# The clamp of the weights' scaled upper words: on GpSimd in place of VectorE, in a fused attention and MLP kernel

## The chip, the cores and the metric

The kernel runs on one core of a Trainium2 chip. The metric is the device time of one execution in microseconds (us), as a median over runs. Five engines work side by side, each through its own instruction queue, in order: TensorE (PE in the rows, PEld for its weight loads), VectorE (DVE), ScalarE (ACT), GpSimd (POOL) and SyncE (SP), which issues the DMAs here.

## The reference

Attention with a narrow band (16 positions to each side) and one summary per block of 32 keys, then an MLP with h * tanh(softplus(h)) over its output. The weights `w_in` (512 x 2048) and `w_out` (2048 x 512) come in as 64-bit floats and have to be made into 32-bit ones.

```python
scores_l = scale * np.matmul(q, k.transpose(0, 1, 3, 2))      # kept where |i - j| < 16
scores_s = scale * np.einsum('bhsd,bhnd->bhsn', q, k_sum) + np.log(32)   # k_sum: maximum of each 32 keys
a = softmax(concatenate([scores_l_m, scores_s]))
x = a @ concatenate([v, v_sum])                               # v_sum: mean of each 32 values
h = x @ w_in
g = h * np.tanh(log1p(exp(h)))
out = g @ w_out
```

q, k and v have shape (4, 8, 768, 64); the MLP works on 3072 tokens of 512 features.

## The kernel before

Tokens are worked on in groups of 512. Attention comes in units (numbered 0, 1, 2, ... after the first ones, a0 to b3), each a pair of heads and 256 tokens: scores on TensorE (`S`), masked maxima on VectorE from PSUM (`ttr`, L380), exponents on ScalarE (`exp`, L393), the divisors (`rs`, L407 and L408), the normalizing product on GpSimd (`nm`, `att_normalize`, L412), a transpose on TensorE (`T`, L418), and the product with the values (`X`, L444). For the scores of a unit GpSimd also copies the block maxima of its keys next to the queries (`kc`, `att_key_summary`, L324).

The MLP runs each product three times on split numbers, upper part and remainder: `ph` (L516) is the first product for one block of 128 hidden features, and needs both words of `w_in`; ScalarE applies the activation and makes the upper part (`ah`, L532), VectorE the remainder (`al`, L534); `po` (L544) is the second product, which needs `ah`, `al` and both words of `w_out`.

The weights come as 16 pieces of 128 x 1024 64-bit words, `w_in` and `w_out` in turn, numbered 0 to 15, and each is turned into 32-bit words by eight steps: `lw` loads it; `f` (L172) scales the upper halves on ScalarE into a tile `w_f` of which there is one; `B` (L176) shifts the lower halves and `C` (L180, the masking) adds the sign bit, both on VectorE and on another tile; `cl` (L184) is the clamp of `w_f`; `E` (L189, the join) brings the two together on VectorE; `hi` (L194) rounds the upper word on ScalarE and `G` (L197) makes the lower word by a subtraction on VectorE. The next piece's `f` waits for `G`, since the tile is free then. The lower words go to `w_early_in`, `w_early_out_lo`, `w_late_in` or `w_late_out_lo`.

The order of the instructions up to about 150 us is a list of words written out by hand, such as

```python
        ... C9 f9 po6 cl9 nm13 lt13 E9 lw11 hi9 pc12 B10
        al7 G9 kc15 f10 ph8 C10 mi8 xl11 ph9 cl10 po7 kc14 mi9 ah8 E10 S14 hi10 ...
```

and each engine takes its instructions in the order in which they stand there. After that stretch the kernel goes on with sums of the weights and products by a seven-product scheme for the later groups; no clamp is left by then.

Of the kernel before, what the change touches and what calls it, by code (L numbers as in the profile page):

```python
# [14 lines left out]
ALU = mybir.AluOpType  # L15
# [48 lines left out]
F32_MAX = (0x47EFFFFF - (OFFSET << 23))  # L64
# [3 lines left out]
def _as_f32(bits):  # L68
    import struct
    return struct.unpack("<f", struct.pack("<I", bits))[0]  # L70
# [3 lines left out]
def fused_kernel(ctx: ExitStack, tc: tile.TileContext, q0, qk, kt, v0, vw, vs, w_in, w_out, out):  # L74
    nc = tc.nc
# [38 lines left out]
    for h in range(2):  # L114
        r = slice(h * QT, (h + 1) * QT)
        nc.gpsimd.affine_select(
            out=base[r, 0:KW], in_=base[r, 0:KW], pattern=[[1, KW]], base=-1,
            channel_multiplier=-1, compare_op=ALU.is_ge, fill=NEG / SCALE)
        nc.gpsimd.affine_select(
            out=base[r, 0:KW], in_=base[r, 0:KW], pattern=[[-1, KW]], base=2 * WIN - 1,  # L120
# [32 lines left out]
    raw, floats = {}, {}  # L153
# [27 lines left out]
                                       op0=ALU.bitwise_and, op1=ALU.bitwise_or)  # L181

    def clamp_weight(k):
        nc.vector.tensor_scalar(out=floats[k], in0=floats[k], scalar1=-_as_f32(F32_MAX), scalar2=_as_f32(F32_MAX),  # L184
                                op0=ALU.max, op1=ALU.min)

    def join_weight(k):
        u = floats[k].bitcast(U32)
# [19 lines left out]
    for part, step, at0 in ((blocks[:, :NW], QT, -WIN), (blocks[:, NW:], P, TG)):  # L208
        n = part.shape[1]
        nc.gpsimd.affine_select(  # L210
            out=part, in_=part, pattern=[[step, n], [-BLK, NB]], base=at0, channel_multiplier=1,
            compare_op=ALU.is_ge, fill=0.0)
        nc.gpsimd.affine_select(
            out=part, in_=part, pattern=[[-step, n], [BLK, NB]], base=BLK - 1 - at0, channel_multiplier=-1,
# [3 lines left out]
        out=part, in_=part, pattern=[[0, NW], [0, NB]], base=-WIN, channel_multiplier=1,  # L218
        compare_op=ALU.is_ge, fill=0.0)
    nc.gpsimd.affine_select(  # L220
        out=part, in_=part, pattern=[[0, NW], [0, NB]], base=WIN + QT - 1, channel_multiplier=-1,
# [461 lines left out]
    def summary_of(name):  # L683
# [10 lines left out]
        "vm": number(first_value_sums), "vc": number(first_value_summary),  # L694
        "lw": number(load_weight), "f": number(scale_weight), "B": number(low_bits), "C": number(sign_bits),
        "cl": number(clamp_weight), "E": number(join_weight), "hi": number(upper_weight),
        "G": number(lower_weight),
        "ph": step(ff_in), "mi": step(ff_act), "ah": split_of, "al": lambda name: lowers.pop("a" + name)(),
# [661 lines left out]
```

## Time and profile before

| | |
|---|---|
| median of 3 runs | 610.29 us (610.21 to 610.61) |
| the profiled execution | 608.81 us, of which the traced span is 606.9 us |
| TensorE busy | 589.2 us (97%) |
| VectorE busy | 452.1 us (75%) |
| ScalarE busy | 386.5 us (64%) |
| GpSimd busy | 80.7 us (13%) |
| granted TensorE clock | 0.996 of 2.4 GHz, mean |

The shares are means over stages with different limits: in the first 140 us, where the weights are made, VectorE is nearly full; later it is not. The rows that follow therefore look at that stretch, at what waits for what in it, and at how the clamp's neighbours stand.

### The profile page before, as it was taken

What the parts mean: (1) busy time and instruction counts of PE and PEld (TensorE: products, weight loads), DVE (VectorE), ACT (ScalarE), POOL (GpSimd) and SP (SyncE); (2) the same over time, 40 slices, a digit from 0 to 9 for tenths busy, and PEclk for the clock granted to TensorE, in tenths of its full rate; (3) what the DMA queues carried; (4) which work ended last, traced back from release to release, by engine and by line L of the source; (5) the groups of instructions that cost most, each with busy time, mean ns of one, the idle gap of its engine ahead of it and who ended that gap; (6) DMA issues with size and microseconds to landing.
All of it is one profiled execution on the core that took longest, in us unless ns stands there. A gap on an engine that the chain in (4) does not pass through costs nothing.

```text
span 606.9 us, 13906 instructions
## 1 busy us (share of the span) xinstructions
PE 589.2 (97%) x5142; PEld 527.4 (87%) x5142; DVE 452.1 (75%) x1158; ACT 386.5 (64%) x990; POOL 80.7 (13%) x119
## 2 busy tenths in 40 slices
PE   3999999999999999999999999999999999999997
PEld 3787777778788888998989898899999999999997
DVE  4999999998677768457786475879488787675565
ACT  3987586785446636588857885885346555666552
POOL 4531211300022012012102210221000000000000
PEclk9899999999999999999999999999999999999999
DMA  9978667653777898398998877697889989797753
GB/s 278 263 258 273 218 194 269 207 198 119 253 267 224 278 301 281 108 370 305 332 350 307 283 259 274 226 322 249 304 307 348 303 300 325 258 335 278 280 183 105
DMA packets 70964, 160.71 MB, mean 265 GB/s; under 512 B 10096, under 2 KB 23152, under 8 KB 70896
## 3 DMA queue, kind: packets, MB, share of 16 engines
q1 hardware_dynamic: 70896, 159.82, 77.8%
q8 instruction: 41, 0.67, 0.5%
q14 instruction: 27, 0.22, 0.1%
HBM read 130.42 MB, written 27.26 MB: 260 GB/s over the span
## 4 chain that ended last, share of the span: by engine, by line
PE 79%; DVE 7%; ACT 2%; issue 1%; DVEq 0%
PE po L544 24%; PE ph L816 14%; PE m L1031 13%; PE inner L1133 12%; PE ph L516 9%; PE x_ps L444 3%; PE pt_ps L418 3%; PE sc L359 3%; DVE w L180 1%; DVE al L534 1%; DVE w L176 1%; DVE w_f L184 1%; DVE w_f L189 1%; DVE w_early_out_lo L197 1%; ACT pr L393 0%
## 5 line engine op out<-in xcount | busy, mean ns | idle before, releaser
L412 POOL TENSOR_TENSOR pr<-pr,rs 128x480 f32<-128x480 f32 x48 | 57.1, 1190 | 278.5 <-DVE rs L408 246.4
L393 ACT ACTIVATE pr<-pr,nm 128x120 f32<-128x120 f32 x192 | 73.8, 388 | 10.3 <-DVE nm L380 10.0
L544 PE MATMUL po<-w_early_out_hi,ah 128*128 128x512 f32 x160 | 63.7, 398 | 0.0
L544 PE MATMUL po<-w_early_out_hi,al 128*128 128x512 f32 x160 | 62.4, 390 | 0.9 <-DVE al L534 0.9
L544 PE MATMUL po<-w_early_out_lo,ah 128*128 128x512 f32 x160 | 62.1, 388 | 0.0
L516 PE MATMUL ph<-xh,w_early_in 128*128 128x512 f32 x160 | 52.0, 391 | 0.0
L534 DVE TENSOR_TENSOR al<-h,ah 128x512 fp32r<-128x512 f32 x32 | 21.8, 690 | 38.3 <-ACT ah L532 38.3
L816 PE MATMUL ph<-xh,w_early_in 128*128 128x256 f32 x272 | 49.3, 276 | 0.0
L1133 PE MATMUL inner<-xh,w_early_in 128*128 128x256 f32 x240 | 49.1, 279 | 0.0
L816 PEld LDWEIGHTS ph<-xh,w_early_in 128*128 128x128 f32 x272 | 42.3, 187 | 0.6
L1133 PEld LDWEIGHTS inner<-xh,w_early_in 128*128 128x128 f32 x240 | 39.5, 187 | 0.1
L544 PE MATMUL po<-w_late_out_hi,ah 128*128 128x512 f32 x96 | 38.3, 399 | 0.0
L523 ACT ACTIVATE a<-ph 128x512 f32<-128x512 f32 x32 | 19.0, 599 | 30.0 <-PE ph L516 29.5
L816 PE MATMUL ph<-xl,w_early_in 128*128 128x256 f32 x136 | 37.4, 275 | 0.0
L544 PE MATMUL po<-w_late_out_lo,ah 128*128 128x512 f32 x96 | 37.3, 388 | 0.0
L544 PE MATMUL po<-w_late_out_hi,al 128*128 128x512 f32 x96 | 37.2, 388 | 0.0
L393 ACT ACTIVATION_READ_ACCUMULATOR pr<-pr,nm 128x1 f32 x192 | 36.6, 190 | 0.0
L544 PEld LDWEIGHTS po<-w_early_out_hi,al 128*128 128x128 f32 x160 | 30.1, 188 | 6.8 <-DVE al L534 2.1
L544 PEld LDWEIGHTS po<-w_early_out_lo,ah 128*128 128x128 f32 x160 | 30.0, 188 | 6.2
L516 PEld LDWEIGHTS ph<-xh,w_early_in 128*128 128x128 f32 x160 | 30.0, 188 | 6.1
L544 PEld LDWEIGHTS po<-w_early_out_hi,ah 128*128 128x128 f32 x160 | 30.0, 188 | 5.6 <-issue 0.8
L380 DVE CUSTOM_DVE_ANT_0 pr<-sc,base 128x120 f32<-128x120 f32 x128 | 31.4, 277 | 4.0 <-PE sc L359 2.6
(268 smaller groups left out, 1711.5 us busy)
## 6 DMA issues: line engine op xcount, KB each, us to landing
w_early_in<-w_sums SPq DMA_DIRECT2D x32, 1024.0 KB
w_early_in<-w_sums SPq DMA_DIRECT2D x32, 768.0 KB
qk<-qk SPq DMA_DIRECT2D x40, 496.0 KB
w<-w_in SPq DMA_DIRECT2D x16, 512.0 KB
w<-w_out SPq DMA_DIRECT2D x16, 512.0 KB
w_sums<-results SPq DMA_DIRECT2D x32, 256.0 KB
vw<-vw SPq DMA_DIRECT2D x40, 192.0 KB
w_late_in<-w_out_sums SPq DMA_DIRECT2D x25, 256.0 KB
```

The source lines that it names most:

```text
L359: nc.tensor.matmul(ps[h][row, at0:at0 + KA], u["qk"][r, s, h * QT:(h + 1) * QT], u["qk"][r, s, P:], start=True, stop=True)
L380: nc.vector.tensor_tensor_reduce(out=pr[:, j, :], in0=ps[h][:, at + pair * KA:at + (pair + 1) * KA], in1=m, scale=-SCALE, scalar=-NEG, op0 ...
L393: nc.scalar.activation(pr[:, s, :], pr[:, s, :], AF.Exp, scale=-1.0, bias=nm[:, s:s + 1], accum_out=sm[:, s:s + 1])
L412: nc.gpsimd.tensor_mul(u["p"], u["p"], u["r"].unsqueeze(2).broadcast_to([P, NQ, KA]))
L418: nc.tensor.transpose(ps[:KA, s * P:(s + 1) * P], u["p"][:, s, :], ident)
L516: nc.tensor.matmul(turned(ph), w[:, cc * P:(cc + 1) * P], turned(x[:, cc, :]), start=(cc == 0 and n == 0), stop=(cc == NCC - 1 and n == 2))
L523: nc.scalar.activation(a, st[g, fc], AF.Mish)
L534: return lambda: nc.vector.tensor_sub(al, a, ah.bitcast(F32))
L544: nc.tensor.matmul(turned(po[g][t]), a[:, tok], turned(w), start=(fc == 0 and n == 0), stop=(fc == NFC - 1 and n == 2))
L816: nc.tensor.matmul(turned(ps), w_[:, a * P:(a + 1) * P], turned(x[:, a, :]), start=(begins and a == 0 and n == 0), stop=(a == 1 and n == 2 ...
L1031: nc.tensor.matmul(turned(ps), a_[:, tok], turned(w_), start=(begins and n == 0), stop=(n == 2), skip_group_check=True)
L1133: nc.tensor.matmul(turned(ps), w_[:, a * P:(a + 1) * P], turned(x[:, a, :]), start=(begins and a == 0 and n == 0), stop=(a == 1 and n == 2 ...
```

## The change

`clamp_weight(k)` is issued on GpSimd in place of VectorE. The two bounds change places: the upper one is applied first. The words of the list stay where they are.

```diff
     def clamp_weight(k):
-        nc.vector.tensor_scalar(out=floats[k], in0=floats[k], scalar1=-_as_f32(F32_MAX), scalar2=_as_f32(F32_MAX),
-                                op0=ALU.max, op1=ALU.min)
+        nc.gpsimd.tensor_scalar(out=floats[k], in0=floats[k], scalar1=_as_f32(F32_MAX), scalar2=-_as_f32(F32_MAX),
+                                op0=ALU.min, op1=ALU.max)
```

On VectorE the 16 clamps leave the queue and nothing else moves. Here is one place, that of piece 3 (`w_2_743` is the tile of its 64-bit words, `w_f` that of the scaled ones):

```order
 L176 TENSOR_SCALAR w_2_743<-w_2_743 128x1024
 L180 SCALAR_TENSOR_TENSOR w_2_743<-w_2_743 128x1024
-L184 TENSOR_SCALAR w_f<-w_f 128x1024
 L189 SCALAR_TENSOR_TENSOR w_f<-w_f,w_2_743 128x1024
 L284 TENSOR_REDUCE km_1_916<-ks_1_852 128x24
```

The masking (L180) and the join (L189) now follow each other; the join still needs the clamp's result.

On GpSimd the clamps come between normalizing products (L412, `pr`) and copies of key maxima (L324, `qk`). Here is the place of clamps 8 to 14; `pr_1_1130` is the product of unit 13, `pr_3_1419` of 15, `pr_2_1408` of 14, and the copies are for units 15, 14, 16 and 17:

```order
+L184 TENSOR_SCALAR w_f<-w_f 128x1024 x2
 L412 TENSOR_TENSOR pr_1_1130<-pr_1_1130,rs_1_1288 128x480
 L324 COPY qk_3_1281<-km_3_1095 128x4x24
+L184 TENSOR_SCALAR w_f<-w_f 128x1024
 L324 COPY qk_2_1222<-km_2_1273 128x4x24
+L184 TENSOR_SCALAR w_f<-w_f 128x1024
 L412 TENSOR_TENSOR pr_3_1419<-pr_3_1419,rs_3_1474 128x480
+L184 TENSOR_SCALAR w_f<-w_f 128x1024
 L324 COPY qk_0_1509<-km_0_793 128x4x24
+L184 TENSOR_SCALAR w_f<-w_f 128x1024
 L412 TENSOR_TENSOR pr_2_1408<-pr_2_1408,rs_2_1512 128x480
 L324 COPY qk_1_1529<-km_1_916 128x4x24
```

The products and copies keep their order among themselves, and each now stands behind the clamps ahead of it: the copy for unit 14 (`qk_2_1222`) behind clamp 10, the product of unit 14 (`pr_2_1408`) and the copy for unit 17 behind clamp 13.

## Rows read from the trace of the kernel before

**Rows 1.** Busy time of each engine in stretches (us), instructions, granted clock, DMA share, GB/s.
```profile
30.00:135.00 105.00, 102.40 (x792) 82.64 (x792) 102.09 (x204) 77.09 (x162) 21.34 (x20) 1.00 0.70 234
135.00:450.00 315.00, 315.00 (x2652) 276.01 (x2649) 222.51 (x633) 198.78 (x521) 44.81 (x60) 1.00 0.79 271
```

**Rows 2.** Waits of TensorE and VectorE, 30 to 135 us: total, times, longest.
```profile
PE po L544 <- DVE al L534: 0.9, 3, 0.4
...
DVE al L534 <- ACT ah L532: 0.8, 2, 0.5
```

**Rows 3.** Timeline: start, duration (us), engine, line, instruction [idle before <- releaser].
```profile
101.55 0.68 DVE L534 TENSOR_TENSOR al<-a,ah 128x512 fp32r<-128x512 f32 x1
102.28 0.49 PE L544 MATMUL po<-w_early_out_hi,al 128*128 128x512 f32 x1 [0.44 <-DVE al L534]
...
121.57 0.72 PE L516 MATMUL ph<-xh,w_late_in 128*128 128x512 f32 x2 [0.46 <-DVE w_late_in L197]
...
133.94 1.42 DVE L197 TENSOR_TENSOR w_late_in<-w_f,w_late_in 128x1024 fp32r<-128x1024 f32 x1
135.81 0.39 PE L516 MATMUL ph<-xh,w_late_in 128*128 128x512 f32 x1
```

**Rows 4.** Timeline: GpSimd beside VectorE at four places.
```profile
23.37 2.91 POOL L412 TENSOR_TENSOR pr<-pr,rs 128x480 f32<-128x480 f32 x2 [3.74 <-DVE rs L407]
25.36 0.94 DVE L284 TENSOR_REDUCE km<-ks 128x24 f32<-128x768 f32 x1
...
59.98 1.96 POOL L324 COPY qk<-km 128x96 f32<-128x96 f32 x2 [6.40 <-DMA qk<-qk]
...
66.41 1.20 DVE L197 TENSOR_TENSOR w_early_out_lo<-w_f,w_early_out_hi 128x1024 fp32r<-128x1024 f32 x1
66.64 1.81 POOL L412 TENSOR_TENSOR pr<-pr,rs 128x480 f32<-128x480 f32 x1 [4.70 <-DVE rs L408]
67.52 1.48 DVE L176 TENSOR_SCALAR w<-w 128x1024 uint32<-128x1024 uint32 x1
```

**Rows 5.** One tile's instructions on GpSimd: shortest, median, longest (ns), first and last start.
```profile
L412 POOL TENSOR_TENSOR pr<-pr,rs x48: 985/987/1967, 14.4 to 415.5; 128x480 f32<-128x480 f32 x48
```

**Rows 6.** Timeline: piece 3 from ScalarE's scaling to the join.
```profile
46.30 1.19 ACT L172 ACTIVATE w_f<-w 128x1024 f32<-128x1024 f32 x1
46.84 0.69 DVE L176 TENSOR_SCALAR w<-w 128x1024 uint32<-128x1024 uint32 x1
47.56 1.23 DVE L180 SCALAR_TENSOR_TENSOR w<-w 128x1024 uint32<-128x1024 uint32 x1
48.71 0.69 DVE L184 TENSOR_SCALAR w_f<-w_f 128x1024 f32<-128x1024 f32 x1
49.43 1.23 DVE L189 SCALAR_TENSOR_TENSOR w_f<-w_f,w 128x1024 uint32<-128x1024 uint32 x1
```

**Rows 7.** GpSimd's groups by shape: count | busy us, mean ns of one | idle before.
```profile
L210 POOL TENSOR_SCALAR_AFFINE_SELECT blocks<-blocks 128x192 f32<-128x192 f32 x1 | 0.4, 397 | 0.1
...
L207 POOL MEMSET blocks<- 128x240 f32 x1 | 0.3, 298 | 0.0
...
L210 POOL TENSOR_SCALAR_AFFINE_SELECT blocks<-blocks 128x48 f32<-128x48 f32 x1 | 0.2, 232 | 0.0
...
L122 POOL MEMSET base<- 128x24 f32 x1 | 0.1, 118 | 0.1
```

**Rows 8.** Timeline: clamps 0 and 13, the product of unit 14, a late second product.
```profile
18.70 1.48 DVE L184 TENSOR_SCALAR w_f<-w_f 128x1024 f32<-128x1024 f32 x1
...
114.36 1.88 POOL L412 TENSOR_TENSOR pr<-pr,rs 128x480 f32<-128x480 f32 x1 [2.05 <-DVE rs L408]
115.31 1.48 DVE L534 TENSOR_TENSOR al<-a,ah 128x512 fp32r<-128x512 f32 x1
...
122.77 0.69 DVE L184 TENSOR_SCALAR w_f<-w_f 128x1024 f32<-128x1024 f32 x1 [0.65 <-ACT w_f L172]
...
147.85 0.49 PE L544 MATMUL po<-w_late_out_hi,ah 128*128 128x512 f32 x1
```

## The prediction

> **What bounds the kernel now.** I read the stretches first, since the clamps lie in the first 140 us alone. From 135 to 450 us TensorE has no idle time at all, so what it loses before 135 us stays lost. From 30 to 135 us TensorE is busy 102.40 and VectorE 102.09 of 105 us [rows 1]: there the two run level, and all but the first two and the last clamp lie there. The question is which of the two the other waits for.
>
> The list of waits answers it: TensorE's largest is the second MLP product waiting for VectorE's `al`, 0.9 us in three waits [rows 2]. The timeline shows where: the product at 102.28 comes just behind the `al` of 101.55 (ended 102.23), the `ph` at 121.57 waits for a lower weight word, and at 135.81 TensorE needs the next lower weight word, which VectorE delivers at 135.36 [rows 3]. The margins are 0, 0 and 0.45 us. Whatever VectorE loses before 135 us is therefore paid by TensorE nearly in full, and what VectorE gains can give back only TensorE's idle time there, 105 - 102.40 = 2.6 us.
>
> **The change part by part.** It takes 16 instructions from VectorE, each worth some 0.65 us from its start to the next one's (0.72 where that one needs its result, as at 48.71 below), and puts 16 on GpSimd, which has the time (21.34 of 105 us busy [rows 1]). The orders of TensorE, ScalarE and SyncE stay, and no DMA is moved. Two things have to be priced: how long GpSimd takes, and what VectorE can do meanwhile.
>
> *VectorE does not go on freely.* A GpSimd product was started at 66.64 during a VectorE subtraction [rows 4]; alone it takes 0.99 us (the median of 48 [rows 5]). It ended at 68.45, which is 0.84 us after the subtraction's end (67.61). The shift that VectorE began at 67.52 took 1.48 us; the one of 46.84 took 0.69 [rows 6]. Two GpSimd copies of 96 elements, which should be shorter than the 397 ns that a selection over 192 takes [rows 7], took 1.96 us together at 59.98, beside VectorE's work on piece 4 and 5 [rows 4]. So a GpSimd instruction and a VectorE one of these kinds exclude each other, with one GpSimd input too, and the one that waits goes next. A GpSimd instruction of length L costs VectorE about L - 0.20 (0.79 for 0.99), and ends about L - 0.15 after VectorE lets go. A VectorE reduction is not held: that of 25.36 took its 0.94 us beside a GpSimd product that ran to 26.28 [rows 4].
>
> The Trainium skill (SBUF — State Buffer, section "Who interferes with whom") says which VectorE instructions are free of this: those with at most one SBUF input, outside the two-port modes. By that page the score maxima and the subtraction from PSUM go on beside a clamp as the reduction does; if they were held too, the sum below would be some 1 us higher. The trace agrees for the reduction.
>
> *The length L of one clamp on GpSimd* has no row. From below: a memset takes 118 ns for 24 elements and 298 for 240, 0.83 ns an element, so 1024 take 0.95 us. From above: the product of two inputs, 987 ns for 480 elements [rows 5], scaled with 0.1 us fixed: 1.99 us. The nearest row reads one tensor, does a little arithmetic and writes one: the selection, 232 ns for 48 elements and 397 for 192, 1.146 ns an element [rows 7]. I take 0.397 + 832 x 0.001146 = 1.35 us.
>
> *Seven clamps (numbers 2, 3, 4, 5, 7, 10, 14) stand in a bare chain.* Number 3 is shown [rows 6]: the scaled words are ready at 47.49, the masking runs from 47.56 to 48.79, the clamp follows, and the join starts at 49.43, 0.64 us after the masking's end. On GpSimd the clamp can run when the masking lets go, ends L - 0.15 later, and the join follows 0.05 us behind (as the `ph` at 121.57 follows VectorE). The join is late by L - 0.15 + 0.05 - 0.64 = 0.61 us. If GpSimd gets in before the masking, the masking is pushed back instead, by about the same. Seven times 0.61 is 4.3 us.
>
> *Four (6, 8, 9, 11) have other VectorE work to run beside them.* There VectorE loses L - 0.20 and saves a step of some 0.65: 0.50 us each, 2.0 us; number 8 less by 0.25, since a subtraction that reads PSUM runs beside it: 1.75 us.
>
> *Numbers 12 and 13.* In GpSimd's order the normalizing product of unit 14 now stands behind clamp 13. Today it runs at 114.36 and stalls the `al` of 115.31 (1.48 us, [rows 8]; that of 101.55 took 0.68). That 0.80 goes away there and comes back ahead of join 13. Today's clamp 13 waits 0.65 us for ScalarE [rows 8]; now the masking that stands behind it in the list fills that wait. The two clamps cost about 0.5 each: -0.80 + 0.80 - 0.65 + 1.0 = +0.35 us.
>
> *Numbers 0 and 1*, before 30 us. Clamp 0 is itself stalled by GpSimd today (1.48 us from 18.70 [rows 8]); VectorE can go on with score maxima that read PSUM. I work out some 0.9 us earlier there, most of it lost again at number 1, where ScalarE's scaling sets the time: -0.2 us.
>
> *Sum.* 4.3 + 1.75 + 0.35 - 0.2 = 6.2 us later for VectorE at 135 us. Of VectorE's own waits for `ah`, 0.8 us in two [rows 2], I let the smaller, 0.3, swallow some (the other is for work that TensorE feeds, and moves along), and 0.45 is the margin at 135.81. That leaves 5.45 us for TensorE. Clamp 15 will be about 1 us late as well, but its words are needed at 147.85 only [rows 8], 12 us behind those of piece 14, while VectorE takes some 7.5 us for a piece (16 pieces in 120 us). Against the profiled execution that is 608.81 + 5.45 = 614.3; the median of the three runs stands 1.48 above that execution, and I add to the median: 610.29 + 5.45 = **615.7 us**. A measurement of this kernel can tell about 0.2% (1.2 us) from no change.
>
> **Rivals.** (a) *The clamp streams at one element a cycle.* With L = 0.95, the bound from the memsets, the terms are 1.5 + 0.15 - 0.45 - 0.2 = 1.0, less 0.75: 0.2 us, 610.5 us, no change that can be told. For it speaks that min and max are light work; against it, that no row with an input comes near that rate. The Trainium skill (GPSIMD Engine Reference, section "Engine selection") calls one-input work on GpSimd roughly line-rate, which is this rival; its section "Elementwise — side-by-side cycle accounting" has 1.8 cycles an element as the best case of a tight loop, from which I estimate 1.54 us for 1024 elements, and by the same terms 618.2 us. No row here has this operation.
>
> (b) *A long clamp, or GpSimd's queue as the new bound.* With L = 1.99 the terms are 8.75 + 4.3 + 1.65 - 0.2 - 0.75 = 13.75: 624 us. The queue alone could do it as well: the copy of the key maxima for unit 14 now stands behind clamp 10, which can't end before about 101.0, while TensorE makes the scores that need it some 2 us before the product at 102.28; and the copy for unit 17 comes after the product of unit 14. By my count the first costs TensorE 0.1 us more than the late `al` does, and the second nothing; if both are dearer, 617 to 618 us.
>
> (c) *Faster.* GpSimd starts when ScalarE's scaling ends and runs beside VectorE instructions that leave it free. Joins then come 0.6 us earlier, and TensorE's 2.6 us of idle time shrink: 607.7 us at best. This needs L below 0.74, or no exclusion; the copies at 59.98 speak against both.
>
> **How the numbers follow.** Forecast (L from 1.1 to 1.65, about 612.5 to 619.5 us) 0.60; (b) 0.18; (a) 0.14; (c) 0.08. The likeliest gives 615.7. The range runs from 610.8, which leaves out (c) and a part of (a), to 621.5, which leaves out the upper part of (b), L above 1.8. By the sign: faster 0.07 and within 0.2% 0.12 from (c) and (a), slower 0.81.
>
> **What would show it.** GpSimd's clamp should take 1.2 to 1.5 us where nothing holds it, and longer by what is left of a masking where it waits. VectorE should be busy less by most of 16 x 0.69 us, and stand waiting for GpSimd ahead of joins, a wait that is absent today. TensorE's idle time from 30 to 140 us should grow from 2.6 to about 8 us, in waits for `al`, `w_late_in` and what follows from them; after 150 us nothing should differ but the offset. I am wrong if the clamp comes out near 0.95 or 2 us, if TensorE's added waits are for GpSimd's copies or products, or if VectorE's subtractions and maskings keep their times while clamps run beside them.

## The result, and the profile after

The changed kernel takes 614.61 us (median of 7 runs, 612.85 to 616.42) against 610.21 us before (7 runs, 609.58 to 610.98). The ratio is 1.0074 [1.0051, 1.0097], so it is slower by 4.4 us; 615.7 was forecast. Its profiled execution took 613.67 us with a span of 611.6 us, 4.86 and 4.7 us more than before.

The clamp itself comes first. This is its line in the profile after (shortest, median, longest in ns, first and last start, form), and who waited for it (total us, times):

```profile
L184 POOL TENSOR_SCALAR w_f<-w_f x16: 1033/1083/1590, 18.8 to 143.0; 128x1024 f32<-128x1024 f32 x16
...
  DVE w_f L189: 8.3, 8
```

Unhindered it takes 1.03 us, not 1.35. The join now waits for it in 8 of 16 pieces.

The stretches and waits that answer to [rows 1, 2], same columns:

```profile
30.00:135.00 105.00, 100.81 (x807) 80.96 (x800) 96.41 (x180) 74.51 (x151) 35.46 (x33) 1.00 0.71 230
135.00:450.00 315.00, 314.75 (x2646) 275.20 (x2643) 221.17 (x636) 200.96 (x529) 47.95 (x63) 1.00 0.80 270
```

```profile
PE po L544 <- DVE al L534: 1.6, 3, 0.8
PE x_ps L444 <- DMA vw<-vm: 1.3, 1, 1.3
PE sc L359 <- POOL qk L324: 1.0, 1, 1.0
...
DVE w_f L189 <- POOL w_f L184: 6.5, 7, 1.3
DVE al L534 <- ACT ah L532: 0.7, 2, 0.4
```

VectorE is busy 5.7 us less than in [rows 1], and stands 6.5 us of that stretch waiting for GpSimd, a wait that was absent. TensorE's idle time grows from 2.6 to 4.2 us, and 0.25 us is new behind 135 us; from 30 to 140 us it is 4.4 us, where the prediction looked for about 8. The wait of 1.3 us that is put down to a DMA stands in a second profile of the changed kernel as one for ScalarE's `a`, also 1.3 us; before, that wait was 0.8 us. So VectorE was relieved of work, and the engine that it feeds still came later.

How much of the 4.7 us of span is the change? The first score and the last addition of the result, first two rows of before, then two of after (start, duration, engine, line, instruction):

```profile
7.81 0.62 PE L363 MATMUL sc<-ks,q 64*64 64x96 f32 x8 [7.81 <-DMA q<-q]
602.61 0.69 DVE L1309 TENSOR_TENSOR results<-inner,x_blocks 128x512 f32<-128x512 f32 x1
```

```profile
8.64 0.62 PE L363 MATMUL sc<-ks,q 64*64 64x96 f32 x8 [8.64 <-DMA q<-q]
606.29 0.69 DVE L1309 TENSOR_TENSOR results<-inner,x_blocks 128x512 f32<-128x512 f32 x1
```

Between the two lie 594.80 us before and 597.65 after: 2.85 us. The first query arrived 0.83 us later in this execution, and the store of the result took 1.0 us longer behind the last addition; neither has a clamp near it. TensorE's added idle time from 30 us on (1.6 and 0.25 us) is not all of the 2.85 us: the join of piece 1, which ends near 33 us, is 0.6 us late already (its rows stand in the section on the prediction).

**A bare chain, piece 4**, answers to [rows 6]:

```profile
56.24 1.22 DVE L180 SCALAR_TENSOR_TENSOR w<-w 128x1024 uint32<-128x1024 uint32 x1
57.03 1.33 POOL L184 TENSOR_SCALAR w_f<-w_f 128x1024 f32<-128x1024 f32 x1 [6.93 <-ACT w_f L172]
58.33 0.98 POOL L412 TENSOR_TENSOR pr<-pr,rs 128x480 f32<-128x480 f32 x1
58.39 2.00 DVE L189 SCALAR_TENSOR_TENSOR w_f<-w_f,w 128x1024 uint32<-128x1024 uint32 x1 [0.93 <-POOL w_f L184]
60.31 0.68 DVE L534 TENSOR_TENSOR al<-a,ah 128x512 fp32r<-128x512 f32 x1
61.05 0.50 PE L544 MATMUL po<-w_early_out_hi,al 128*128 128x512 f32 x1 [0.84 <-DVE al L534]
```

The clamp is started at 57.03 while the masking runs, and ends at 58.36, 0.90 us after the masking (57.46), which is L - 0.13. The join follows 0.03 us behind: 0.93 us from the masking's end where it was 0.64, late by 0.29, that is L - 0.74. What was not in that term is the next row: the product that was queued behind the clamp goes next, and the join needs 2.00 us in place of 1.23. TensorE then waits for `al`. This stall is moved rather than new: in the kernel before, the same product ran at 52.28 and held the subtraction of piece 3 (2.00 us from 52.66, in place of some 1.2).

**Piece 3**, where GpSimd gets in ahead of the masking:

```profile
49.06 1.04 POOL L184 TENSOR_SCALAR w_f<-w_f 128x1024 f32<-128x1024 f32 x1 [6.62 <-ACT w_f L172]
49.15 2.03 DVE L180 SCALAR_TENSOR_TENSOR w<-w 128x1024 uint32<-128x1024 uint32 x1
51.28 1.23 DVE L189 SCALAR_TENSOR_TENSOR w_f<-w_f,w 128x1024 uint32<-128x1024 uint32 x1
52.42 0.95 DVE L284 TENSOR_REDUCE km<-ks 128x24 f32<-128x768 f32 x1
```

The masking takes 2.03 us instead of 1.23 [rows 6]: 0.80, or L - 0.24, against 0.72 that the clamp used to take there. The reduction, which would have run beside the clamp, stands behind the join.

The sum over the pieces, from the groups of lines from 30 to 145 us (count | busy us, mean ns of one | idle us before them, and what ended it), before and then after:

```profile
L189 DVE SCALAR_TENSOR_TENSOR w_f<-w_f,w 128x1024 uint32<-128x1024 uint32 x15 | 18.6, 1239 | 0.4
L180 DVE SCALAR_TENSOR_TENSOR w<-w 128x1024 uint32<-128x1024 uint32 x14 | 17.8, 1272 | 0.2
...
L184 DVE TENSOR_SCALAR w_f<-w_f 128x1024 f32<-128x1024 f32 x14 | 10.4, 744 | 0.8 <-ACT w_f L172 0.7
```

```profile
L180 DVE SCALAR_TENSOR_TENSOR w<-w 128x1024 uint32<-128x1024 uint32 x14 | 21.7, 1552 | 0.2
L189 DVE SCALAR_TENSOR_TENSOR w_f<-w_f,w 128x1024 uint32<-128x1024 uint32 x15 | 21.5, 1434 | 8.8 <-POOL w_f L184 8.3
```

VectorE is spared 10.4 us of clamps and 0.8 of waits ahead of them. It pays 3.9 us in maskings, 2.9 in joins and 8.4 in waits. The balance is 4.0 us against it, of which part is stalls by products that used to fall on other instructions, such as the one at piece 4.

### The profile page after: what moved, and what is told of

Its sections match the earlier page's. It is cut to its first block, busy times and chain, and to the rows that moved or that the text cites. A ratio compares the mean times of both kernels' runs of the same rounds, so it can differ in the third digit from the quotient of the medians.

```text
span 611.6 us, 13912 instructions
## 1 busy us (share of the span) xinstructions
PE 589.6 (96%) x5142; PEld 526.9 (86%) x5142; DVE 446.4 (73%) x1142; ACT 386.6 (63%) x990; POOL 97.9 (16%) x135
## 4 chain that ended last, share of the span: by engine, by line
PE 77%; DVE 5%; issue 3%; ACT 2%; POOL 1%; POOLq 0%; DVEq 0%; ACTq 0%
PE po L544 23%; PE ph L816 13%; PE m L1031 12%; PE inner L1133 12%; PE ph L516 8%; PE x_ps L444 3%; PE pt_ps L418 3%; PE sc L359 2%; POOL w_f L184 1%; DVE w L180 1%; ACT w_f L172 1%; DVE al L534 1%; DVE w_f L189 1%; DVE w L176 1%; ACT pr L393 0%
## 5 line engine op out<-in xcount | busy, mean ns | idle before, releaser
L412 POOL TENSOR_TENSOR pr<-pr,rs 128x480 f32<-128x480 f32 x48 | 54.8, 1142 | 234.5 <-DVE rs L408 209.9
L523 ACT ACTIVATE a<-ph 128x512 f32<-128x512 f32 x32 | 19.0, 595 | 30.7 <-PE ph L516 30.2
```

Of the source, the lines that this page charges most:

```text
L412: nc.gpsimd.tensor_mul(u["p"], u["p"], u["r"].unsqueeze(2).broadcast_to([P, NQ, KA]))
L523: nc.scalar.activation(a, st[g, fc], AF.Mish)
```

## The experiments

**First: how long may the clamp be?** Theory: the clamp shuts VectorE out for about L - 0.2 us, and what counts is whether that is more or less than the 0.65 us that the step takes on VectorE. Rival: GpSimd's queue, or something that comes with the change whatever L is. Four kernels on one chip: the change once more, without the clamp (it is left out, the words go on unclamped), with the clamp made twice, and on one half of the columns (the other half stays unclamped).

```diff
 def clamp_weight(k):          # change once more: as it is
-    nc.gpsimd.tensor_scalar(out=floats[k], in0=floats[k], ...)
+    pass                                                            # without
+    nc.gpsimd.tensor_scalar(...); nc.gpsimd.tensor_scalar(...)      # twice
+    nc.gpsimd.tensor_scalar(out=floats[k][:, :WP], in0=floats[k][:, :WP], ...)  # half
```

> The changed kernel once more, with a second profile. In the first one GpSimd's clamp took 1.03 us where nothing held it (1.35 was taken), TensorE's first instruction began 0.83 us later than in the profile of before, its last one lay 2.84 us more behind the first, and the stretch after the last addition was 1.1 us longer. Theory (the two engines exclude each other, VectorE loses about 0.3 us at a bare chain): first to last again 2.5 to 3.2 us longer than before, the rest of the difference is chance of the first loads and the last stores, so the median is 612.5 to 614.5. Rival (TensorE's granted clock falls for longer because of the new waits): a profile with more half-clock time, first to last over 4 us longer.

> The clamp is left out on both engines. Theory (VectorE and TensorE run level from 30 to 135 us): VectorE has 16 steps of some 0.65 us less to do, and TensorE gives back most of its 2.6 us of idle time: 607.5 to 608.7 us, a ratio of 0.996 to 0.9975. Rival (VectorE has slack, and only the waits for GpSimd cost): 610 us, no change.

> Each clamp is made twice on GpSimd, one right behind the other; the second changes nothing in the values. L goes from 1.03 to about 2.0 us. Theory (VectorE's loss grows by all of what GpSimd's clamp grows by, at some 13 of 16 places): 11 to 13 us over the changed kernel, 624 to 628 us. Rival (a fixed cost of handing the tile from engine to engine, or of the moved products and copies): at most 5 us more, under 619 us.

> Only 512 of the 1024 columns are clamped, on GpSimd; the others are left unclamped. L falls to about 0.6 us, under the 0.74 us at which the chain breaks even. Theory (L decides): at or a little faster than before, 608.3 to 610.2 us. Rival (a fixed cost of handing over): still 612 us or more.

| kernel | one clamp, shortest (us) | median (us) | ratio to before | us against before |
|---|---|---|---|---|
| no clamp | 0 | 606.32 | 0.9940 [0.9916, 0.9963] | -3.7 |
| half of the columns | 0.608 | 609.33 | 0.9976 [0.9955, 0.9998] | -1.5 |
| before (VectorE, 0.69) | | 610.73 | 1 | 0 |
| the change | 1.034 | 613.08 | 1.0050 [1.0032, 1.0069] | +3.1 |
| twice | 2 x 1.04 | 627.40 | 1.0274 [1.0254, 1.0294] | +16.7 |

The last column is the ratio less 1, times 610.73. The lines of the half clamp and of the second clamp, and TensorE's largest wait from 30 to 135 us with two clamps:

```profile
L184 POOL TENSOR_SCALAR w_f<-w_f x16: 608/625/1355, 18.7 to 142.3; 128x512 f32<-128x512 f32 x16
```

```profile
L186 POOL TENSOR_SCALAR w_f<-w_f x16: 1039/1041/1895, 20.1 to 158.3; 128x1024 f32<-128x1024 f32 x16
...
PE po L546 <- DVE al L536: 6.0, 4, 2.8
```

The time goes with L and changes its sign on the way. Between half and whole it rises by 4.5 us for 0.425 us of L, and passes the time of before, on a straight line between the two, at 0.608 + 1.5 / 4.5 x 0.425 = 0.75 us (0.62 to 0.86 by the ends of the intervals). The chain's arithmetic put this point at 0.74. A cost that comes whatever L is can't be large, since the half clamp, with the same places in the queue and the same kind of wait, is quicker than before. A queue's cost could still grow with L; that is for the second set. From one clamp to two the time grows by 13.6 us for 1.04 us of L, as if 13 of the 16 places paid in full, which is about what was expected. The times of the change, the half clamp and the clamp made twice all lie in their expected ranges. The second profile of the change bears the first out: from the first score to the last addition it has 597.44 us, 2.64 more than before. The kernel without the clamp gained more than expected. TensorE then has no idle time at all from 30 us on, which is 2.6 us, and in the profiled pair piece 1 is already 0.7 us earlier, counted from the first score:

```profile
30.00:135.00 105.00, 105.00 (x827) 85.98 (x819) 97.79 (x197) 80.61 (x170) 22.62 (x21) 1.00 0.73 241
```

So the 16 clamps cost this kernel 3.7 us on VectorE, and 6.7 on GpSimd.

**Second: is it GpSimd's queue, or what VectorE has to do meanwhile?** One kernel sets three products and one copy that now stand behind clamps ahead of them again. One moves VectorE work that should not be held (reductions, score maxima, subtractions from PSUM) to where VectorE stands still for seven of the clamps, ahead of the masking or of the join; its control has the same order and the clamp on VectorE. One does both.

```diff
# queue back
-C4 cl4 E4 mi2 al1 hi4 nm10 ... cl9 nm13 ... cl10 po7 kc14 ... nm15 cl12 ... dv15 nm14 kc17
+C4 nm10 cl4 E4 mi2 al1 hi4 ... nm13 cl9 ... kc14 cl10 po7 ... nm15 nm14 cl12 ... dv15 kc17
# filled (four of the seven places)
-cl2 E2 pcb3 hi2 S10 xl2 ... C3 exp11 ph2 cl3 xh9 mi0 E3 km13 ... cl5 E5 lqk13 lqk12 lt12 hi5 vq12
+cl2 xl2 E2 pcb3 hi2 S10 ... km13 C3 exp11 ph2 cl3 xh9 mi0 E3 ... cl5 lqk13 lqk12 lt12 vq12 E5 hi5
-cl7 C7 exp12 E7 pc11 exp13 lt15 vq15
+cl7 lt15 vq15 C7 exp12 E7 pc11 exp13
...
# control: as filled, and
-        nc.gpsimd.tensor_scalar(out=floats[k], in0=floats[k], scalar1=_as_f32(F32_MAX), scalar2=-_as_f32(F32_MAX),
-                                op0=ALU.min, op1=ALU.max)
+        nc.vector.tensor_scalar(out=floats[k], in0=floats[k], scalar1=-_as_f32(F32_MAX), scalar2=_as_f32(F32_MAX),
+                                op0=ALU.max, op1=ALU.min)
```

> The changed kernel, with GpSimd's products of units 10, 13 and 14 and the copy for unit 14 put back ahead of clamps 4, 9, 12 and 10; nothing else moves. Theory (exclusion, whoever's turn it is): the copy's wait on TensorE (1.0 us at 104) goes away but the stalls only change places: 0 to 0.8 us faster than the changed kernel, 612.2 to 613.1 us. Rival (GpSimd's queue is the new bound): 2 us or more faster, 611 or less.

> The changed kernel, with VectorE instructions that read at most one tensor in SBUF (key maxima, value sums, a remainder from PSUM, score maxima) moved to where VectorE stands still for clamps 2, 3, 5, 6, 7, 12 and 14; no other engine's order changes. Theory (exclusion holds two-input and two-port instructions alone, so these run beside the clamp): VectorE gets back 0.4 to 1.2 us at each, some 5 us by 121 us, so TensorE's last instruction comes 3 to 5 us earlier than in the changed kernel: 608.5 to 610.5 us. Rival (everything on VectorE is held by a clamp, or the moved work only delays the joins): 612.5 us or more.

> The same reordering in the kernel before, with the clamp on VectorE: the control. Theory: VectorE has the same work and no holes to fill, so no gain: ratio 0.999 to 1.002. Rival (the order itself was worth something): 0.997 or less.

> Both reorderings together on the changed kernel. Theory: VectorE's work is less by what runs beside the clamps, and TensorE's waits of 30 to 140 us go below the 2.6 us of before: 607.5 to 609.5 us, faster than before by 0.2 to 0.4%, the bound being the 606.3 us without a clamp. Rival: as e5.

Queue back: 612.89 us, ratio 1.0040 [1.0019, 1.0061], within the interval of the change as it is and inside what was expected. TensorE's waits from 30 to 135 us no longer name GpSimd, and others have grown in their place:

```profile
PE po L544 <- DVE al L534: 2.3, 4, 0.9
PE x_ps L444 <- ACT a L523: 1.3, 1, 1.3
PE ph L516 <- DVE w_late_in L197: 0.8, 1, 0.8
```

TensorE's idle time there is 4.65 us, no less than the 4.2 of the change as it is. So for these four places the queue is where the loss shows, not where it comes from.

Filled: 613.56 us, 1.0045 [1.0029, 1.0061]; with both, 613.77, 1.0052 [1.0034, 1.0069]. Both missed what I expected. So did the control, with VectorE's clamp: 614.72, 1.0068 [1.0049, 1.0087]. So the new order alone costs 4 us, and on it GpSimd's clamp is not the slower one. The filled order's rows show both halves of this. At piece 3 the reduction runs beside the clamp at its full speed, and the masking loses little (compare with piece 3 above). At piece 7 the reduction `vq` of unit 15 comes too early for its transfer, and VectorE stands still for 3.1 us ahead of 82.31 (2.6 in the control). This wait swamps what the filling could give, so these three kernels say little on that:

```profile
49.59 0.95 DVE L284 TENSOR_REDUCE km<-ks 128x24 f32<-128x768 f32 x1
49.62 1.04 POOL L184 TENSOR_SCALAR w_f<-w_f 128x1024 f32<-128x1024 f32 x1 [6.72 <-ACT w_f L172]
50.46 1.29 DVE L180 SCALAR_TENSOR_TENSOR w<-w 128x1024 uint32<-128x1024 uint32 x1
```

```profile
DVE w_f L189 <- POOL w_f L184: 5.8, 6, 1.9
...
DVE vq L309 <- DMA vsum<-vs: 3.1, 1, 3.1
```

**Third: exclusion alone, and a few clamps only.** In the first of these the clamp of `w_f` is left out, and at the places of clamps 3 to 13 GpSimd clamps another tile of the same size that nobody waits for: the join has nothing to wait for, and only the exclusion is left. (One GpSimd copy fills that tile first.) Then four clamps on GpSimd where the order was filled (2, 3, 5, 6), its control with all clamps on VectorE, and three (2, 3, 6) with the order of piece 5 as before.

```diff
+        if not 3 <= k <= 13:
+            return
+        other = piece(15, 1)
+        if k == 3: nc.gpsimd.tensor_copy(other, ...)
-        nc.gpsimd.tensor_scalar(out=floats[k], in0=floats[k], ...)
+        nc.gpsimd.tensor_scalar(out=other, in0=other.bitcast(F32), ...)
...
# four; with three k in (2, 3, 6); the control is the kernel before with the order of four
+        on_gp = k in (2, 3, 5, 6)
+        (nc.gpsimd if on_gp else nc.vector).tensor_scalar(out=floats[k], in0=floats[k], ...)
```

> The clamp of the scaled words is left out, and GpSimd clamps a tile of its own size that nobody waits for, at the places of clamps 3 to 13. The join waits for nothing; what is left is the exclusion. Theory (each such instruction takes about 0.83 us from VectorE unless a spared instruction runs beside it): 11 times up to 0.83, 5 to 9 us on VectorE, so 607.5 to 610 us, 2 to 3.5 us above the 606.3 us without a clamp. Rival (VectorE loses by waiting for the clamp's result only): 606 to 606.8 us, as without a clamp.

> Only clamps 2, 3, 5 and 6 are on GpSimd, each with a VectorE instruction that the exclusion spares moved to where the clamp runs; the other twelve stay on VectorE, and the vq sum of unit 15, which waited 3 us for its load in the run with seven moved instructions, stays in its place. Theory: VectorE saves 4 steps of some 0.65 us, less 0.2 at clamp 2: 2.4 us by 75 us, and TensorE's idle time takes up most of it: 608 to 609 us, ratio 0.996 to 0.998. Rival (what TensorE waits for between 60 and 80 us is not VectorE): 610 us or more.

> The control for the four: the same places in the list, all clamps on VectorE. Theory: the sum of unit 12 and the maxima of unit 15 now stand ahead of the joins and masking, so joins 5 and 6 are about 1 us later: ratio 1.000 to 1.003, at least 1.5 us above the four on GpSimd. Rival (the order is what helps): as fast as the four on GpSimd.

> Clamps 2, 3 and 6 on GpSimd with the spared instructions moved beside them; piece 5 is as before, since its late join made ScalarE, and behind it TensorE at 69 us, 0.7 us later in the run with four. Theory: VectorE saves some 1.7 us by 75 us without a late join, and TensorE gains 0.5 to 1.5 us: 609 to 610 us, ratio 0.997 to 0.9995. Rival (nothing but VectorE's whole load counts, or ScalarE is next): 1.000 or more.

Apart: 612.39 us, 1.0032 [1.0015, 1.0048], which is 0.92% or 5.6 us above the kernel without any clamp (measured on another chip), for 11 clamps. I had expected 607.5 to 610. Its rows show VectorE held without any data between the two engines: an `al` of 0.68 us takes 1.53, a masking 2.06.

```profile
71.02 2.92 POOL L189 TENSOR_SCALAR w_late_out_lo<-w_late_out_lo 128x1024 fp32r<-128x1024 f32 x2
71.52 1.53 DVE L539 TENSOR_TENSOR al<-a,ah 128x512 fp32r<-128x512 f32 x1
72.97 2.06 DVE L180 SCALAR_TENSOR_TENSOR w<-w 128x1024 uint32<-128x1024 uint32 x1
```

The groups from 30 to 145 us tell what this sums to, in the kernel without any clamp and then here:

```profile
L180 DVE SCALAR_TENSOR_TENSOR w<-w 128x1024 uint32<-128x1024 uint32 x14 | 17.9, 1277 | 0.2
...
L533 DVE TENSOR_TENSOR al<-a,ah 128x512 fp32r<-128x512 f32 x16 | 13.1, 822 | 2.3 <-ACT ah L531 2.1
```

```profile
L180 DVE SCALAR_TENSOR_TENSOR w<-w 128x1024 uint32<-128x1024 uint32 x15 | 21.5, 1432 | 0.2
...
L539 DVE TENSOR_TENSOR al<-a,ah 128x512 fp32r<-128x512 f32 x14 | 13.8, 989 | 1.1 <-ACT ah L537 1.1
```

Shifts, joins, subtractions and divisors are longer too; each group's added mean times its count here makes some 8 us for the 11 clamps, and the joins wait no longer than in the kernel without. So the exclusion alone is enough for a loss of this size on VectorE, the 5 to 9 us that I had expected there; the kernel paid more for it than expected. It doesn't part exclusion and wait exactly: a clamp that nobody waits for starts at other moments, and TensorE's largest wait in this kernel is 1.7 us for a copy on GpSimd, which is its queue again.

Four: 611.52 us, 1.0007 [0.9987, 1.0026]; its control 612.11, 1.0035 [1.0018, 1.0051]; three: 609.91, 0.9997 [0.9984, 1.0011]. I had expected 608 to 609 us for four and 609 to 610 for three, both with ratios below 0.9995, and the control at 1.000 to 1.003. The median of four lies 1.6 us above that of before (609.92), more than its ratio says, and its executions lie 5.7 us apart; against its control the intervals overlap. Where reductions fill the gap, a clamp on GpSimd costs nothing that can be told, and gives nothing either. No version here beats the kernel before, except those that leave work out.

## Why the prediction was right, and where it was not

**The level run and the sign: right.** VectorE's delay is paid by TensorE: counted from the first score, the lower word of piece 14 is 2.99 us later than before (the row below against that of 133.94 in [rows 3]), and the last addition 2.85. After 150 us nothing but the offset differs.

```profile
137.76 1.42 DVE L197 TENSOR_TENSOR w_late_in<-w_f,w_late_in 128x1024 fp32r<-128x1024 f32 x1
```

The prediction had 6.2 us for VectorE at this place, twice as much. Two of its own signs of being wrong are also near: the clamp is nearer to 0.95 than to 1.35 us, and one of TensorE's added waits, 1.0 us, is for a GpSimd copy. The exclusion is shown by the clamp that nobody waits for, and its two figures by the rows: L - 0.24 for a masking, L - 0.13 until the clamp's end.

**The Trainium skill** (SBUF — State Buffer, section "Who interferes with whom") says that the lock lasts a whole instruction and that a VectorE reduction is free of it on this chip. The traces agree on both: 0.95 us for the reduction beside a clamp, 2.03 for the masking. The prediction's reading of it for score maxima holds too: in the second profile of the change they take 0.28 us each from 19.10 on, while clamp 0 runs from 18.68 to 20.06.

**L was mis-sized: 1.03 in place of 1.35.** The step that failed was to take the selection as the nearest row. The half clamp gives the slope: (1033 - 608) / 512 = 0.83 ns a column, just that of the memsets [rows 7], and 0.18 us fixed. So it is the lower bound's rate; only the fixed part, 0.10 us in that bound, is 0.08 larger. The Trainium skill's "roughly line-rate" for one input (GPSIMD Engine Reference, section "Engine selection") is what the trace bears out; the 1.54 us estimated from its best case of 1.8 cycles an element ("Elementwise — side-by-side cycle accounting") is not.

**The reliefs were too generous, and this made up for half of it.** With L = 1.035 the terms give seven times 0.295, four times 0.185 less 0.25, two times 0.185 less 0.65, and -0.2: 2.08, less 0.75 that waits and margin were to swallow, 1.3 us. Measured are 2.85 us in the profiled pair and 3.1 in the second comparison. The chain terms without any relief (2.07 + 0.74 + 0.37 = 3.2) are nearer. The reliefs can be followed in the profiled pair. Numbers 0 and 1 were to gain 0.2 us. Join 1, before and then after:

```profile
30.77 1.48 DVE L189 SCALAR_TENSOR_TENSOR w_f<-w_f,w 128x1024 uint32<-128x1024 uint32 x1
```

```profile
30.62 1.03 POOL L184 TENSOR_SCALAR w_f<-w_f 128x1024 f32<-128x1024 f32 x1
31.63 0.98 POOL L412 TENSOR_TENSOR pr<-pr,rs 128x480 f32<-128x480 f32 x1
31.69 2.00 DVE L189 SCALAR_TENSOR_TENSOR w_f<-w_f,w 128x1024 uint32<-128x1024 uint32 x1
```

Counted from the first score it starts at 23.05 in place of 22.96, and ends 0.6 us later, mostly since the product behind the clamp holds it: 0.8 us off. Between join 1 and the lower word of piece 14 VectorE loses 2.99 - 0.6 = 2.4 us, and the terms of pieces 2 to 14 make 2.08 + 0.2 = 2.28: in sum they hold, though not piece by piece (the stall that moved from subtraction 3 to join 4 is one reason). Waits for `ah` swallowed 0.1 us (0.8 before, 0.7 now), not 0.3. The margin of 0.45 at 135.81 swallowed nothing, since TensorE had been late long before it: ScalarE's activation of a first product (L523) that starts at 110.05 before starts at 113.72 now, 2.84 us later counted from the first score. The prediction had itself found no margin at 102.28. That accounts for the whole: 0.8 for numbers 0 and 1, 0.1 for pieces 2 to 14, 0.6 of the 0.75.

So 615.7 came out near by luck in good part. The mis-sized L put in 4.1 us too much (13 clamps by 0.315 us), the rest was some 1.5 too little, and the first comparison came out 1.3 us above the second. The two intervals overlap, and the executions of one kernel lie some 4 us apart.

**The rivals.** (a) had L nearly right (0.95 for 1.03) and its time wrong by 2.5 to 4 us, largely because its terms carried the same reliefs. (b) had the one place right: the copy for unit 14 behind clamp 10 holds TensorE,

```profile
102.96 1.04 POOL L184 TENSOR_SCALAR w_f<-w_f 128x1024 f32<-128x1024 f32 x1 [3.03 <-ACT w_f L172]
103.95 0.26 POOL L324 COPY qk<-km 128x96 f32<-128x96 f32 x1
104.27 1.05 PE L359 MATMUL sc<-qk 64*64 64x120 f32 x32 [0.96 <-POOL qk L324]
```

but the kernel with that copy and three products put back is no quicker by what can be told, and the wait for the next `al` takes its place. Its long clamp was the kernel with two: 627.4. (c) asked for L below 0.74 or no exclusion. The half clamp has such an L and is indeed quicker, by 1.5 us; the whole one is above it.

## What to carry to other kernels

In this kernel moving a step of 0.65 to 0.72 us from VectorE to an idle GpSimd would have paid only below some 0.75 us on GpSimd, that is, where GpSimd's time less 0.1 to 0.2 us is below what the step costs VectorE. That holds as long as VectorE has nothing but work of the kinds that were held here (maskings, joins, shifts, subtractions of two tensors in SBUF) to run beside it; the idle share of GpSimd says nothing about it. Look at what is queued on GpSimd behind the moved step too: it goes next, and holds the instruction that waited for the step. Move work only to where its own inputs are there: one early sum cost 3 us. And price an unknown operation from the simplest row of its engine plus a fixed part, then test it by halving its size, which shows the price and the break-even point at once.

## What was not expected of the hardware

Two clamp operations on one 32-bit tensor cost GpSimd 0.83 ns a column, no more than a memset, and 0.18 us fixed. And a VectorE instruction over 4 columns, which takes 0.16 us alone, is held as fully as a large one. This one stood beside a GpSimd product that ran to 30.66 in the changed kernel:

```profile
28.78 1.88 POOL L412 TENSOR_TENSOR pr<-pr,rs 128x480 f32<-128x480 f32 x1 [2.08 <-DVE rs L408]
...
29.73 0.95 DVE L407 TENSOR_SCALAR rs<-sm 128x4 f32<-128x4 f32 x1
```

TensorE's granted clock is not the same in every execution of one kernel. The first 30 us of the changed kernel, as profiled first and then again:

```profile
0.00:30.00 30.00, 17.80 (x359) 15.55 (x363) 18.17 (x87) 18.97 (x74) 14.47 (x40) 0.94 0.95 255
```

```profile
0.00:30.00 30.00, 17.17 (x384) 14.84 (x384) 19.55 (x87) 19.69 (x75) 13.79 (x40) 1.00 0.96 262
```

The kernel before has 0.94 there too. By estimate 0.94 over 30 us is some 3.6 us at the lower level of 1.2 GHz, in which at most 1.8 us of work are lost. In this pair little of that reached the end: from the first score to the last addition the two lie 0.21 us apart. Such a stretch came later too, in the control of the filled order. There TensorE was busy for 1.83 of the 4.00 us before it, at a granted clock of 1.00, with a wait of 1.8 us for ScalarE's `a`:

```profile
73.20:76.60 3.40, 3.40 (x11) 2.63 (x10) 3.20 (x11) 0.95 (x1) 0.00 (x0) 0.54 0.01 2
```

The filled order loses without it: its profile on GpSimd has a granted clock of 1.00 up to 450 us, and that execution took 614.01 us. Whether such stretches are why executions of one kernel scatter by some us is not shown.
